# Transposing q in 64x64 tiles instead of 64x128 tiles, in a kernel of linear attention and channel mix on one core

## The chip, the cores and the metric

The kernel runs on one core of a Trainium2 chip. The metric is the time of one execution on the device in microseconds (us); lower is better. Names used below: PE is the matrix engine (TensorE), with its weight loads shown apart as PEld; DVE is VectorE, ACT is ScalarE, POOL is GpSimd, SP is SyncE, which only issues transfers here. SBUF is the on-chip memory that all engines read; PSUM is the small memory that PE writes its results to, in banks; a tile of PSUM must be copied out by ACT or DVE.

A matmul on PE has a weight load (LDWEIGHTS), which puts one operand into the 128x128 array, and the matmul proper (MATMUL), which moves the other operand through it. Operands of 64 rows or 64 columns use only a part of the array, a tile: 64x128 is one half of the rows and all columns, 64x64 a quarter. A transpose is a matmul with the identity as the moving operand.

## What is computed

```python
# q, k, v: (8 batches, 8 heads, 576 tokens, 64)
q_s = softmax(q, over the 64)
k_s = softmax(k, over the 576 tokens)
kv  = k_s^T v                  # 64 x 64 for each batch and head
x   = q_s kv                   # heads joined: (8, 576, 512)
# channel mix; x_prev is x one token back
xk, xr = mu_k * x + (1 - mu_k) * x_prev, mu_r * x + (1 - mu_r) * x_prev
out = sigmoid(xr w_r) * (relu(xk w_k)^2 w_v)   # w_k 512 x 1024, w_v 1024 x 512
```

Inputs and output are float32; inside the kernel the matmuls take bfloat16.

## The kernel before

**Head groups.** The attention is done in sixteen head groups, eight batches (b) of two (g). Each group has four heads: r = 0, 1 lies in the two halves of the 128 partitions of q, k and v (64 partitions each, tokens in the partitions, nine runs of 64 tokens each, j = 0 to 8), and u = 0, 1 is a second index beside it. For a group, ACT takes the exponentials of q and k (L383) and casts v (L389); DVE sums q's (L398), inverts (L402) and scales (L407), which gives the tile qs with 128 columns for each j: the 64 features of u = 0, then the 64 of u = 1.

**On PE, one operation for a group of batches 1 to 7** (`block`, L505) issues, one behind the other:
- X (L591): the product x = q_s kv of the group before, in 64x64 tiles, eight matmuls: four of 64 columns, four of 512. It is there in the blocks from the second group of batch 2 on; batches 0 and 1 get their x in another way (L550).
- T (L417): the transposes of qs, 18 of them, each of 64 rows (r) by 128 columns (both u), into a PSUM half for each r.
- KV (L444): the sums kv, 36 matmuls in 64x64 tiles: for each j, then u, then r, with a column of ones beside v that gives the sum of k's exponentials.

In batch 0, T (L417) and KV (L438 and L441) are operations of their own.

Behind a block, DVE inverts the sums of k (L451) and scales kv (L461), then ACT copies the transposed q out of PSUM to the tile qt (L424). X of this group stands in the next block and waits for that copy. What X writes is copied out by ACT (L597, L600) and mixed with its shift by DVE (L605 to L619).

**The channel mix** is the bulk of PE's work, in matmuls of the full 128x128 array, mostly 512 columns wide: K (L687, xk with w_k), R (L719, xr with w_r) and V (L739, the squares with w_v), four or so to a group of instructions. ACT takes relu (L672) and tanh (L724) out of PSUM, DVE squares (L676) and forms the output (L745), SP stores it (L757).

**Order.** All engines get their instructions in one order, found when the kernel is built: `Plan.order` walks through all operations with their assumed lengths and latencies, takes for each engine what can start first, and among those what is due first; buffers of a pool are handed out on the way. A block's assumed length is a constant in the code (1.1 us, or 0.9 without X), which the change leaves as it is. On the chip each engine goes through its order and waits by semaphores for what an instruction needs. PSUM has four banks "mm" for the channel mix and two pairs of banks "att" for the attention.

Of the kernel before, what the change touches and what calls it, by code (L numbers as in the profile page):

```python
# [81 lines left out]
class Plan:  # L82
# [6 lines left out]
    def add(self, engine, occ, lat, key, emit, deps=(), takes=(), gives=(), size=0.0, rate=1.0,  # L89
            name=""):  # L90
        op = Op(engine, occ, lat, key, emit, [d for d in deps if d is not None], takes, gives,
                size, rate, name)
        self.ops.append(op)
        return op
# [141 lines left out]
def graph(kn):  # L236
# [5 lines left out]
    def in_turn(name):  # L242
        slot = Slot(name)
        slot.rank = ranks.get(name, 0)
        ranks[name] = slot.rank + 1
        return slot
# [59 lines left out]
    identity = add("POOL", 0.6, 0.8, -9.1, lambda: make_identity(kn.nc, kn.ident[:]))  # L306
# [63 lines left out]
    def attention(b, g):  # L370
# [3 lines left out]
        eq, ek, vv, stat, qs, qt, rz = (  # L374
            in_turn(n) if n != "vv" or b else None
            for n in ("eq", "ek", "vv", "stat", "qs", "qt", "rz"))
# [3 lines left out]
        two = (slice(0, 64), slice(64, 128))  # L380
# [30 lines left out]
        def turned(slot, hf):  # L411
            return kn.half(slot, hf).bitcast(BF16)[:, 0:S]

        def transpose_q(slot):
            for j in range(J):
                for r in range(2):
                    kn.nc.tensor.transpose(out=turned(slot, r)[:, 64 * j:64 * j + 64],  # L417
                                           in_=kn.qss[qs.index][two[r], j, :],
                                           identity=kn.ident[two[r], two[r]])

        def copy_qt(slot):
            to = kn.qts[qt.index]
# [72 lines left out]
        if b == 0:  # L495
            qtp, kvp = Slot("any"), Slot("any")
            tr = add("PE", 0.6, 0.7, step, lambda: transpose_q(qtp), before_t, [qtp], [qs],
                     name=f"T{tag}")
            kvm = add("PE", 0.9, 1.0, step, lambda: kv(kvp), before_kv + [tr], [kvp], leave_kv,
                      name=f"KV{tag}")  # L500
        else:
            qtp = kvp = Slot("att")
            turn_x = pending.pop() if pending else None

            def block():  # L505
                if turn_x:
                    turn_x[0](qtp)
                transpose_q(qtp)
                kv(qtp)

            if turn_x:
                tr = kvm = add("PE", 1.1, 1.25, step, block, before_t + before_kv + turn_x[1],
                               [qtp] + turn_x[2], [qs] + leave_kv + turn_x[3], name=f"B{tag}")
                tr.look = BLOCK_LOOK
                turn_x[4](tr, qtp)
            else:
                tr = kvm = add("PE", 0.9, 1.0, step, block,
                               before_t + before_kv + (fused_x if not fused else []), [qtp],
                               [qs] + leave_kv, name=f"TKV{tag}")
# [391 lines left out]
```

## Time and profile before

| | |
|---|---|
| median of 3 runs | 206.15 us (205.49 to 206.4) |
| the profiled execution | 205.87 us |
| its span, first to last instruction | 204.1 us |
| granted clock of PE | 0.995 of full speed |
| busy in the span: PE / DVE / ACT / POOL | 92% / 75% / 72% / 19% |
| T, median of one transpose and of one weight load (L417) | 190 ns, 95 ns |
| KV, median of one matmul and of one weight load (L444) | 192 ns, 107 ns |

The profile is of one execution. Busy time is the time in which an engine has at least one instruction under way; matmuls overlap, so the length of one says little about how many fit into a microsecond, and the distance between starts says more. In a line of the timeline stand the start and the length of a run of like instructions, the engine, the line of the code, the operation, the tile written and the tiles read, the part of the array (rows*columns), the shape of the moving operand and the count. Line numbers are those of the kernel before.

### The profile page before, as it was taken

What the parts mean: (1) busy time and instruction counts of PE and PEld (TensorE: products, weight loads), DVE (VectorE), ACT (ScalarE), POOL (GpSimd) and SP (SyncE); (2) the same over time, 40 slices, a digit from 0 to 9 for tenths busy, and PEclk for the clock granted to TensorE, in tenths of its full rate; (3) what the DMA queues carried; (4) which work ended last, traced back from release to release, by engine and by line L of the source; (5) the groups of instructions that cost most, each with busy time, mean ns of one, the idle gap of its engine ahead of it and who ended that gap; (6) DMA issues with size and microseconds to landing.
All of it is one profiled execution on the core that took longest, in us unless ns stands there. A gap on an engine that the chain in (4) does not pass through costs nothing.

```text
span 204.1 us, 4851 instructions
## 1 busy us (share of the span) xinstructions
PE 187.9 (92%) x1930; PEld 93.9 (46%) x1930; DVE 152.7 (75%) x348; ACT 146.8 (72%) x226; POOL 38.6 (19%) x61
## 2 busy tenths in 40 slices
PE   0659999979999999999999999999999999999990
PEld 0445444534454444444466444444444444444750
DVE  1865478999889989999999995999825459622620
ACT  4463689999999999999999488777624752642520
POOL 4912269433223312532000000000000000000000
PEclk9999999999999999999999999999999999999997
DMA  6999999999999994999742220422044012404303
GB/s 206 277 247 206 256 404 391 399 405 405 392 393 400 410 385 137 368 348 401 224 102 53 48 58 3 100 57 53 0 100 110 0 41 65 103 0 103 90 16 104
DMA packets 16431, 40.10 MB, mean 197 GB/s; under 512 B 2196, under 2 KB 5528, under 8 KB 16408
## 3 DMA queue, kind: packets, MB, share of 16 engines
q0 software_dynamic: 9328, 27.99, 41.6%
q1 hardware_dynamic: 6696, 11.25, 19.7%
q10 hardware_dynamic: 384, 0.56, 0.8%
q8 instruction: 15, 0.25, 0.5%
q14 instruction: 8, 0.07, 0.1%
HBM read 33.56 MB, written 9.44 MB: 211 GB/s over the span
## 4 chain that ended last, share of the span: by engine, by line
PE 78%; DMA 13%; DVE 3%; ACT 2%; POOL 1%; issue 0%; DVEq 0%; ACTq 0%
PE mm_b L739 9%; PE mm_c L739 9%; PE mm_d L739 7%; PE mm_b L687 7%; DMA wr<-in_moe_w_r_dram 7%; PE mm_c L687 7%; PE mm_d L687 7%; PE mm_a L687 7%; PE mm_a L719 6%; DMA raw_g<-in_v_dram 4%; PE mm_a L739 4%; PE mm_d L719 3%; PE mm_c L719 3%; PE mm_b L719 3%; DMA raw_b<-in_q_dram 2%; PE att_b L444 1%
## 5 line engine op out<-in xcount | busy, mean ns | idle before, releaser
L687 PEld LDWEIGHTS <-wk_a 128*128 128x128 bf16 x160 | 15.3, 99 | 17.0 <-issue 1.8
L687 PEld LDWEIGHTS <-wk_b 128*128 128x128 bf16 x160 | 15.5, 98 | 15.3 <-issue 0.2
L719 PEld LDWEIGHTS <-xr 128*128 128x128 bf16 x144 | 13.9, 98 | 16.8 <-ACT xr L563 0.9
L739 PEld LDWEIGHTS <-k_a 128*128 128x128 bf16 x144 | 13.8, 98 | 16.4
L739 PEld LDWEIGHTS <-k_b 128*128 128x128 bf16 x152 | 14.2, 98 | 14.7 <-issue 0.2
L719 PE MATMUL mm_a<-wr,xr 128*128 128x512 bf16 x56 | 14.4, 379 | 0.4 <-DMA raw_g<-in_v_dram 0.4
L724 ACT ACTIVATE th_a<-mm_a 128x512 f32<-128x512 f32 x14 | 8.4, 602 | 7.2 <-PE mm_a L719 7.1
L687 PE MATMUL mm_b<-xk,wk_a 128*128 128x512 bf16 (+1 forms) x44 | 11.2, 371 | 0.0
L687 PE MATMUL mm_c<-xk,wk_a 128*128 128x512 bf16 (+1 forms) x40 | 10.2, 371 | 0.0
L687 PE MATMUL mm_a<-xk,wk_a 128*128 128x512 bf16 (+1 forms) x40 | 9.8, 360 | 0.3 <-DVE xk L560 0.3
L687 PE MATMUL mm_c<-xk,wk_b 128*128 128x512 bf16 (+1 forms) x40 | 9.4, 358 | 0.0
L687 PE MATMUL mm_d<-xk,wk_b 128*128 128x512 bf16 (+1 forms) x40 | 9.4, 358 | 0.0
L687 PE MATMUL mm_a<-xk,wk_b 128*128 128x512 bf16 (+1 forms) x40 | 9.4, 358 | 0.0
L687 PE MATMUL mm_b<-xk,wk_b 128*128 128x512 bf16 (+1 forms) x40 | 9.4, 358 | 0.0
L687 PE MATMUL mm_d<-xk,wk_a 128*128 128x512 bf16 (+1 forms) x36 | 9.2, 368 | 0.0
L315 PE MATMUL mm_a<-mu_rows,pick 2*128 2x512 f32 x2 | 2.0, 1122 | 6.8 <-DMA mu_rows<-in_moe_mu_r_dram 6.8
L719 PE MATMUL mm_d<-wr,xr 128*128 128x512 bf16 x32 | 8.2, 379 | 0.0
L719 PE MATMUL mm_b<-wr,xr 128*128 128x512 bf16 x28 | 7.2, 379 | 0.0
L719 PE MATMUL mm_c<-wr,xr 128*128 128x512 bf16 x28 | 7.2, 379 | 0.0
L676 DVE TENSOR_TENSOR k_a<-rel_a 128x512 bf16<-128x512 bf16 (+1 forms) x13 | 5.1, 391 | 2.8 <-ACT rel_a L672 2.6
L672 ACT ACTIVATE rel_b<-mm_a 128x512 bf16<-128x512 f32 (+1 forms) x7 | 4.0, 571 | 4.1 <-PE mm_a L687 3.9
L676 DVE TENSOR_TENSOR k_a<-rel_c 128x512 bf16<-128x512 bf16 (+1 forms) x13 | 5.1, 392 | 2.4 <-ACT rel_c L672 2.3
(323 smaller groups left out, 487.7 us busy)
## 6 DMA issues: line engine op xcount, KB each, us to landing
out_dram<-ot_a SPq DMA_DIRECT2D x14, 128.0 KB, 2.4
out_dram<-ot_b SPq DMA_DIRECT2D x14, 128.0 KB, 2.4
out_dram<-ot_c SPq DMA_DIRECT2D x14, 128.0 KB, 3.2
out_dram<-ot_d SPq DMA_DIRECT2D x14, 128.0 KB, 2.7
raw_k<-in_v_dram POOLq DMA_DIRECT2D x3, 576.0 KB, 8.5
out_dram<-ot_e SPq DMA_DIRECT2D x13, 128.0 KB, 2.4
raw_j<-in_k_dram POOLq DMA_DIRECT2D x2, 576.0 KB, 10.7
raw_a<-in_q_dram POOLq DMA_DIRECT2D x2, 576.0 KB, 10.1
```

Of the source, the lines that this page charges most:

```text
L315: nc.tensor.matmul(kn.bank(wide_slot), lhsT=kn.pick[:].rearrange("p u c -> p (u c)"), rhs=kn.mu_rows[:].rearrange("p m c -> p (m c)"), sta ...
L444: kn.nc.tensor.matmul(to, lhsT=by, rhs=kn.vvs[vv.index][two[r], j, u, 0:65], **flags)
L672: kn.nc.scalar.activation(out=kn.rels[rel.index][:, 0:n], in_=kn.bank(kf)[:, 0:n], func=ACT.Relu, scale=HALF_ROOT)
L676: kn.nc.vector.tensor_tensor(out=kn.k2s[k2.index][:, fc, 0:n], in0=kn.rels[rel.index][:, 0:n], in1=kn.rels[rel.index][:, 0:n], op=ALU.mult)
L687: kn.nc.tensor.matmul(kn.bank(kf)[:, 0:n], lhsT=kn.wk[fc // 4][:, ct, (fc % 4) * 128:(fc % 4) * 128 + 128], rhs=kn.xs[0][:, ct, c0:c0 + n] ...
L719: kn.nc.tensor.matmul(kn.bank(rps), lhsT=kn.xs[1][:, ct, c:c + 128], rhs=kn.wr[:, ct, :], start=(ct == 0), stop=(ct == CT - 1))
L724: kn.nc.scalar.activation(out=kn.ths[th.index][:], in_=kn.bank(rps), func=ACT.Tanh, scale=0.5)
L739: kn.nc.tensor.matmul(kn.bank(vps)[:, 0:width], lhsT=kn.k2s[k2.index][:, ft, 128 * m:128 * m + 128], rhs=kn.wv[ft // 4][:, ft % 4, part], ...
```

## The change

```diff
         def transpose_q(slot):
             for j in range(J):
-                for r in range(2):
-                    kn.nc.tensor.transpose(out=turned(slot, r)[:, 64 * j:64 * j + 64],
-                                           in_=kn.qss[qs.index][two[r], j, :],
-                                           identity=kn.ident[two[r], two[r]])
+                for u in (two if b else (slice(0, 128),)):
+                    for r in range(2):
+                        kn.nc.tensor.transpose(
+                            out=turned(slot, r)[u, 64 * j:64 * j + 64],
+                            in_=kn.qss[qs.index][two[r], j, u],
+                            identity=kn.ident[two[r], two[r]])
```

`two` is the pair of slices 0 to 63 and 64 to 127. In batches 1 to 7 each transpose of 64x128 becomes two of 64x64, one for each half of the columns; for each j the four follow each other with r as the inner index, as KV's four do. Batch 0 keeps the 64x128 tiles. The result in PSUM is the same, at the same place. PE gets 252 transposes and 252 weight loads more (14 groups, 18 of each); the order of operations and the buffers are those of before on every engine.

## The prediction

> **What bounds the kernel now.** I read the page first, then TensorE's (PE's) waits, then the order of PE's work around one block, and last what ACT does at the same time. The page gives the busy time of each engine and the chain that ended last:
>
> ```profile
> PE 187.9 (92%) x1930; PEld 93.9 (46%) x1930; DVE 152.7 (75%) x348; ACT 146.8 (72%) x226; POOL 38.6 (19%) x61
> PE 78%; DMA 13%; DVE 3%; ACT 2%; POOL 1%; issue 0%; DVEq 0%; ACTq 0%
> ```
>
> The chain is 78% PE; in order of time it is PE alone from 43.2 us to 198.9 us. The view of waits for PE between 50 and 200 us is empty. So a stretch taken out of PE's stream behind 50 us ends the run earlier, unless another engine then makes PE wait. One block, by PE's timeline (start, length, engine, line, operation, tiles, array rows*columns, shape, count):
>
> ```profile
> 59.49 1.03 PE L739 MATMUL mm_d<-wv_b,k_b 128*128 128x512 bf16 x4
> 60.45 0.22 PE L591 MATMUL att_a<-qt_b,w_b 64*64 64x64 bf16 x4
> 60.50 0.39 PE L591 MATMUL att_b<-qt_b,w_b 64*64 64x512 bf16 x4
> 60.82 0.44 PE L417 MATMUL att_a<-ident,qs_a 64*128 64x64 bf16 x18
> 61.19 0.48 PE L444 MATMUL att_a<-vv_b,ek_a 64*64 64x65 bf16 x36
> 61.60 1.04 PE L739 MATMUL mm_b<-wv_a,k_b 128*128 128x512 bf16 x4
> 62.47 1.03 PE L719 MATMUL mm_c<-wr,xr 128*128 128x512 bf16 x4
> ```
>
> The starts matter, since the lengths overlap. L591 is the product x of the former head group (X), L417 the transposes (T), L444 the kv sums (KV). Three things are read from it.
> - **A change of tile costs 0.09 us.** Four 512-column matmuls take 0.865 us (0.216 each), but from the V group at 59.49 to X it is 0.96: 0.095 more. In the single records the last 512-column matmul of X starts at 60.512 and T at 60.824: 0.312, again 0.095 over 0.216. The last pair of T starts at 61.070 and KV at 61.190: 0.120, where a pair follows a pair in 0.029: 0.091. KV to V: 0.12 likewise. Within the 64x64 tile, from X's 64-column to its 512-column matmuls, no such gap stands, nor at 16.32, where batch 0's x product (288 columns, 64x64) is followed by its kv sums (64x64) 0.227 behind, less than the 0.24 in which these products follow each other there (15.37, 15.61, 15.85).
> - **T's step.** Two transposes, one for each row half, start every 0.029 us; 9 steps.
> - **KV's step.** Four 64x64 matmuls with four weight loads start every 0.032 us on average (8 steps in 0.276, the first of them 0.052, while the next weights come in); 36 matmuls in all.
>
> ACT beside it (the same columns):
>
> ```profile
> 58.17 1.20 ACT L389 CAST vv_b<-raw_h 128x1152 bf16<-128x1152 f32 x1
> 59.22 1.16 ACT L424 COPY qt_b<-att_b 128x1152 bf16<-128x1152 bf16 x1
> 60.23 0.65 ACT L724 ACTIVATE th_a<-mm_a 128x512 f32<-128x512 f32 x1
> ```
>
> X at 60.45 reads qt_b, whose copy ended at 60.38: 0.07 us ahead. ACT is then as full as PE. The windows (length, PE, PEld, DVE, ACT, POOL busy) say for how long:
>
> ```profile
> 50.00:61.00 11.00, 11.00 (x188) 5.32 (x182) 9.81 (x21) 11.00 (x16) 3.27 (x5) 1.00 1.03 392
> 61.00:109.00 48.00, 48.00 (x515) 24.26 (x508) 46.67 (x100) 47.38 (x68) 11.58 (x16) 1.00 0.84 299
> 109.00:198.00 89.00, 89.00 (x722) 43.10 (x720) 59.42 (x134) 52.05 (x85) 0.00 (x0) 1.00 0.24 56
> ```
>
> Until 109 us ACT and DVE have next to nothing left; behind it ACT has 37 us free.
>
> **The change, part by part.** Fourteen head groups (batches 1 to 7, two each) get 36 transposes and 36 weight loads in place of 18 and 18. Nothing else is added, moved or made to wait; ACT, DVE, POOL and SP keep their instructions and order.
> 1. *T's own stream.* A step now holds four 64x64 tiles: two row halves by two column halves, in KV's order, with loads of KV's size and moving rows of 64 columns against its 65. Bounds: 0.029 a step (today's pair) and 0.058 (two pairs, one behind the other). I take KV's 0.032, the same instructions but for the transpose: 9 x 0.032 = 0.288 against 9 x 0.029 = 0.261 today and 0.01 more at T's start, so +0.02.
> 2. *X to T.* Both are 64x64: 0.312 becomes about 0.21. -0.10.
> 3. *T to KV.* Both 64x64: the 0.091 goes. KV's long first step (0.052) becomes 0.032, as its weights load behind T: -0.02.
> 4. KV to the next matmul stays at 0.12.
>
> A block with X in front: 0.10 + 0.09 + 0.02 - 0.02 = 0.19 to 0.20; I take 0.20. Of these there are 11 (55.74, 60.45, 70.34, 77.63, 95.29, 101.72, 115.97, 125.85, 129.70, 137.00, 161.56). Without X in front (52.23, and 35.99 and 38.60 in batch 1) the start change of tile stays, and the long first step moves to T: 0.09 + 0.02 - 0.02 - 0.01 = 0.08. The bound for a switch is zero (it stays, rival 1) to the whole 0.19.
>
> The weight loads are the point that speaks against the change:
>
> ```profile
> L417 PEld LDWEIGHTS <-qs_a x108: 92/95/129, 10.3 to 162.2; 64*128 64x128 bf16 x108
> L444 PEld LDWEIGHTS <-ek_c x180: 102/107/111, 36.4 to 138.0; 64*64 64x64 bf16 x180
> ```
>
> A load of half the columns takes 107 ns against 95, and there are twice as many. They overlap, so KV's step, not these lengths, is the price. [...]
>
> *What reaches the end.*
> - Before 50 us PE waits for others (the batch 1 blocks at 35.99 and 38.60 are followed, at 43.16, by a PE wait of 1.2 us for an ACT copy of xk): nothing, whichever way.
> - 50 to 61: 0.08 from 52.23 is kept, since ACT's tanh at 54.08 waits for the R group behind it, and the copy of qt_a that X at 55.74 needs follows on ACT. The 0.20 of the block at 55.74 is lost: X at 60.45 waits for qt_b, and ACT runs from 54.08 to there without a gap. 0.08 left.
> - 61 to 109: five blocks, 1.0 offered. At 108.09 PE needs the bank that ACT's relu at 107.43 (0.40 long) frees, 0.26 ahead. So PE is earlier there by 0.26 more than ACT. ACT is earlier by at least its 0.08, plus what it had itself waited: 0.2 in the waits view (for DVE's w_c) and short waits for matmuls at 72.6, 91.9 and 94.5 that I put at 0.2. PE: 0.34 to 1.1; I take 0.7.
> - 109 to the end: five blocks, 5 x 0.20 = 1.0. The nearest wait is X at 125.85, 0.19 behind a copy that itself follows PE. Kept.
>
> Sum: 0.7 + 1.0 = 1.7 us. The profiled execution took 205.87 (span 204.1 and 1.8 around it), so 204.2; it lay 0.28 below the median of 206.15, on which basis it is 204.4. Bounds of this case: 1.3 (only 0.34 kept by 109) to 2.4 (no wait binds), 203.7 to 204.9.
>
> **The rivals.**
> 1. *The drain belongs to the change between transpose and product, not to the tile.* No row shows a transpose next to a product of the same tile. Then nothing goes and T's step costs +0.03 a block: 12 x 0.03 = +0.4, 206.5. Against it: changes of tile without a transpose (V to X, KV to V) cost the same 0.095, and T's two switches no more.
> 2. *ACT and DVE take more of it.* Blocks to 109 give 0 and one or two later ones are lost at X (slacks of 0.19 at 125.85, 0.55 at 129.70): gain 0.4 to 1.0, 205.4. For it: the full ACT above. Against: 37 us of room behind 109.
> 3. *The instructions do not come fast enough* (the slower side). From X to the end of KV PE starts 160 instructions where there were 124 in 1.03 us (8.3 ns each); the forecast wants them in 0.83, 5.2 ns each. Batch 0's kv sums hold 6.6 ns over 144 (four every 0.053 us, at half today's pace), KV 4 ns over 72 only, which a buffer may have held. If the supply were 8.3 ns, a block takes 1.33: +0.3, 12 times, +3.6: 209.8. It decides from 6.4 ns on, where 160 take today's time.
>
> ```profile
> 13.98 0.26 PE L438 MATMUL att_b<-vb_a,ek_a 64*64 64x64 bf16 x4
> 14.03 0.21 PE L441 MATMUL att_a<-one,ek_a 64*64 64x1 bf16 x4
> 14.09 0.26 PE L438 MATMUL att_b<-vb_a,ek_a 64*64 64x64 bf16 x4
> ```
>
> 4. *The added transposes stand in line.* If the column halves do not run side by side, a step is 0.058: T 0.52, a block 0.03 slower than now even without the drains, 206.5; with each of the 18 alone at 0.029, 0.3 slower, 209.8. Against it: KV's four tiles start 0.0035 apart. [...]
>
> **How the numbers follow.** Half a percent, 1.0 us, is about what a measurement of this kernel can tell from no change. Forecast 0.64 (all of it faster), rival 1 0.13 and rival 2 0.09 (same), rival 3 0.08 (slower), rival 4 0.06 (half same, half slower). Faster 0.64, same 0.25, slower 0.11. The range takes in the forecast's bounds, rivals 1 and 2 and the mild half of 4: 203.6 to 206.6.
>
> **What would show it.** Right: the transposes as 64*64 x36, T 0.22 behind X's 512 columns (now 0.32), KV 0.29 behind T (now 0.37), the next group 0.39 behind KV (now 0.41), and new PE waits for ACT near 60 and 108 us. Wrong: 0.31 and 0.12 still standing around T (rival 1), T's step above 0.055 (rivals 3 and 4), or a block 0.20 shorter with the end less than 1 us earlier (rival 2).

## The result, and the profile after

The changed kernel takes 207.56 us in the median of 20 runs (206.53 to 211.04), the kernel before 206.01 (204.92 to 206.84). The ratio is 1.0071, 95% interval 1.0048 to 1.0094: slower by 1.5 us, where 1.7 us less was forecast. Four runs of over 210 us, with a granted clock of 0.982 to 0.983 against 0.984 to 1.000 in the others, are left out of the ratio. The profiled execution took 207.04 us (span 205.3).

The page's busy times and chain:

```profile
PE 183.7 (90%) x2158; PEld 94.0 (46%) x2182; DVE 152.2 (74%) x348; ACT 146.7 (71%) x226; POOL 38.5 (19%) x61
PE 49%; issue 1%; ACT 0%; DVE 0%
```

The kernel has 2182 matmuls, one for each weight load, and 2158 of them are recorded; the 24 that are missing leave short gaps in the view (0.16 us) that are no waits. The chain is PE alone again, but is lost half way back, at a place without a releaser.

The blocks did what was forecast of them, the end did not. PE's timeline of one block, in the columns of the view before:

```profile
61.93 1.03 PE L741 MATMUL mm_d<-wv_b,k_b 128*128 128x512 bf16 x4
62.88 0.22 PE L593 MATMUL att_a<-qt_b,w_b 64*64 64x64 bf16 x4
62.94 0.39 PE L593 MATMUL att_b<-qt_b,w_b 64*64 64x512 bf16 x4
63.16 0.48 PE L418 MATMUL att_a<-ident,qs_a 64*64 64x64 bf16 x36
63.45 0.49 PE L446 MATMUL att_a<-vv_b,ek_a 64*64 64x65 bf16 x36
```

T starts 0.22 behind X's 512 columns where it was 0.32, KV 0.29 behind T where it was 0.37. But one block earlier the same view shows this:

```profile
56.81 0.37 PE L418 MATMUL att_b<-ident,qs_c 64*64 64x64 bf16 x20
57.00 0.45 PE L446 MATMUL att_b<-vv_a,ek_c 64*64 64x65 bf16 x32
59.17 0.22 PE L446 MATMUL att_b<-vv_a,ek_c 64*64 64x65 bf16 x4 [1.72 <-issue]
```

Of KV's 36 matmuls 32 are issued, then PE stands for 1.9 us between two weight loads (57.23 to 59.17), in the middle of an operation that waits for nothing. In the square brackets stand the idle time and its releaser; "issue" means that the profile knows none. PE's waits, largest first:

```profile
PE mm_a L315 <- DMA mu_rows<-in_moe_mu_r_dram: 7.5, 1, 7.5
PE att_b L446 <- issue: 1.7, 1, 1.7
PE att_a L443 <- ACT qt_a L426: 1.0, 1, 1.0
PE att_a L552 <- DVE wp_a L540: 1.0, 1, 1.0
```

The first and third were there before. The second is the standstill just shown. The fourth is new as well: a product of batch 1 (L552) that starts at 42.36 where it started at 41.21. PE's row for it, and DVE's for what it reads:

```profile
42.36 0.44 PE L552 MATMUL att_a<-qt_c,wp_b 64*64 64x288 bf16 x8 [0.96 <-DVE wp_a L540]
```

```profile
38.46 0.90 DVE L540 TENSOR_TENSOR wp_b<-kvn_a,mu_wide 128x128 bf16<-128x128 f32 x4
39.66 0.20 DVE L534 COPY qt_c<-qt_c 128x126 bf16<-128x126 bf16 x1 [0.31 <-ACT qt_c L426]
```

It reads wp_b and qt_c, not wp_a; they were done at 39.36 and 39.86, 2.5 us ahead. The releaser named is only what ended last on DVE by then.

**What stands at both places** shows in the number of the instruction. Counting PE's weight loads and matmuls from the start of the program (two instructions for each weight load, since each has its matmul), PE stops behind the 956th and behind the 1468th: 512 apart. The trace's DMA records hold instruction transfers as packets of 16,384 bytes on queue 8 (the page's "q8 instruction": 15 packets before, 17 after, for 504 instructions more, some 250 to a packet). The author's estimate is 256 to a packet, from the 512 between the two stops if two packets lie between them; 956 is then 444 + 2 x 256 and 1468 is 444 + 4 x 256. So if 444 instructions are there at the start, the third packet brings the 957th instruction and the fifth the 1469th. The 444 is chosen to fit these two places. The count leaves out PE's other instructions (waits on semaphores, for one), so that it gets rougher with every packet. From those records (us):

```
                        packet 3 landed   next instr.   packet 5 landed   next instr.
before                  40.79             44.44         57.83             61.38
changed                 41.13             42.36 stood   57.83             59.17 stood
```

Before, PE came to these instructions 3.6 us behind their packets. The changed kernel comes there earlier and goes on 1.2 to 1.3 us after the packet has landed. By this reading PE had run out of instructions; the experiments test it.

### The profile page after: what moved, and what is told of

It is laid out like the page before. It is cut to its first block, busy times and chain, and to the rows that moved or that the text cites. A ratio compares the mean times of both kernels' runs of the same rounds, so it can differ in the third digit from the quotient of the medians.

```text
span 205.3 us, 5331 instructions
## 1 busy us (share of the span) xinstructions
PE 183.7 (90%) x2158; PEld 94.0 (46%) x2182; DVE 152.2 (74%) x348; ACT 146.7 (71%) x226; POOL 38.5 (19%) x61
## 4 chain that ended last, share of the span: by engine, by line
PE 49%; issue 1%; ACT 0%; DVE 0%
PE mm_c L741 7%; PE mm_b L741 6%; PE mm_b L689 5%; PE mm_c L689 4%; PE mm_d L741 4%; PE mm_a L689 4%; PE mm_d L689 4%; PE mm_a L721 3%; PE mm_a L741 3%; PE mm_d L721 3%; PE mm_b L721 2%; PE mm_c L721 1%; PE att_a L593 1%; PE att_b L593 1%; PE att_b L446 1%
## 5 line engine op out<-in xcount | busy, mean ns | idle before, releaser
L689 PE MATMUL mm_d<-xk,wk_a 128*128 128x512 bf16 (+1 forms) x34 | 8.7, 367 | 0.3 <-issue 0.3
L674 ACT ACTIVATE rel_c<-mm_a 128x512 bf16<-128x512 f32 (+1 forms) x7 | 4.0, 567 | 4.3 <-PE mm_a L689 4.3
L678 DVE TENSOR_TENSOR k_a<-rel_b 128x512 bf16<-128x512 bf16 (+1 forms) x14 | 5.7, 405 | 1.7 <-ACT rel_b L674 1.6
```

Source lines behind the costliest of these rows:

```text
L674: kn.nc.scalar.activation(out=kn.rels[rel.index][:, 0:n], in_=kn.bank(kf)[:, 0:n], func=ACT.Relu, scale=HALF_ROOT)
L678: kn.nc.vector.tensor_tensor(out=kn.k2s[k2.index][:, fc, 0:n], in0=kn.rels[rel.index][:, 0:n], in1=kn.rels[rel.index][:, 0:n], op=ALU.mult)
L689: kn.nc.tensor.matmul(kn.bank(kf)[:, 0:n], lhsT=kn.wk[fc // 4][:, ct, (fc % 4) * 128:(fc % 4) * 128 + 128], rhs=kn.xs[0][:, ct, c0:c0 + n] ...
```

## The experiments

The theory after this (supply): the added instructions bring PE to the end of its stock before the next packet is usable, because the packets come slowly behind the loads of q, k and v. The rival (tile): 64x64 transposes disturb PE where they stand. Each edit is to the changed kernel, unless said otherwise.

**e1_from2 and e8_from2_again: 64x64 from batch 2 on.**

```diff
-                for u in (two if b else (slice(0, 128),)):
+                for u in (two if b >= 2 else (slice(0, 128),)):
```

> 64x64 transposes from batch 2 on; batch 1 keeps 64x128, as batch 0 does, so 36 loads and 36 matmuls fewer than the changed kernel. Supply theory: PE ran out of instructions twice in the changed kernel's profile (1.0 us at its 956th, 1.9 us at its 1468th load-or-matmul instruction), because batch 1's and 2's extra instructions brought those points forward to before the next 16 KB of instructions had come. With 72 fewer, both points come later than the fetch: no stall, every block about 0.2 us shorter, 203.8 to 205.0 where before is 206.0. Tile theory (64x64 transposes disturb PE wherever they stand in a dense stretch): eleven of the blocks are as they were, so the time stays near 207.5, at most 0.3 less.

> 64x64 transposes from batch 2 on, again, on the chip of the last kernel for the comparison: 1.0 to 1.4 us faster than the kernel before, no stall.

Measured: 204.31 us against 205.35 (ratio 0.9943, 0.9923 to 0.9963), and again 204.18 against 205.66 (0.9934, 0.9911 to 0.9957). PE's waits have no line of "issue" and none for wp_a; in e1's profile the packets land at 40.40 and 56.74, and PE comes to the two places at 43.90 and 60.11, 3.5 and 3.4 us behind them. The second place now lies in the T of this block, which runs through:

```profile
59.86 0.41 PE L593 MATMUL att_b<-qt_b,w_b 64*64 64x512 bf16 x4
60.08 0.49 PE L418 MATMUL att_a<-ident,qs_a 64*64 64x64 bf16 x36
60.39 0.49 PE L446 MATMUL att_a<-vv_b,ek_a 64*64 64x65 bf16 x36
```

All eleven blocks with X are as in the changed kernel, so the tile theory is wrong. What was taken back is 36 weight loads and 36 transposes, in two groups that PE had to wait behind anyway.

**e2_only12: 64x64 in batches 1 and 2 only.**

```diff
-                for u in (two if b else (slice(0, 128),)):
+                for u in (two if b in (1, 2) else (slice(0, 128),)):
```

> 64x64 transposes in batches 1 and 2 only. Supply theory: the same two stalls as in the changed kernel and next to none of the gain (0.1 to 0.3 us): 207.5 to 209.5. Tile theory: four of fourteen blocks changed, so about four fourteenths of the 1.5 us: 206.3 to 206.6, and no stall that stands out at the 956th and 1468th instruction.

Measured: ratio 1.0160 (1.0110 to 1.0211), by the three of six runs that took 207.2 to 209.7 us; the other three took 211.7, 212.1 and 253.4, and the profile is of the first of these. PE stood behind the 956th and the 1468th instruction again (1.85 and 2.10 us from one weight load to the next).

**e3_pad12: the old tiles, each transpose of batches 1 and 2 issued twice.**

```diff
-                for u in (two if b else (slice(0, 128),)):
+                for u in (slice(0, 128),) * (2 if b in (1, 2) else 1):
```

> The tiles of the kernel before (64x128 everywhere), but in batches 1 and 2 each transpose is issued twice, which writes the same values again: as many instructions as with 64x64 tiles there, no change of tile saved, and T 0.26 us longer in each of four blocks, of which two lie where PE is not the bound. Supply theory: the two stalls of the changed kernel appear without any 64x64 transpose, 207.5 to 210. Tile theory: no stall, 206.1 to 206.6.

Measured: 208.47 us, ratio 1.0145 (1.0111 to 1.0178). PE's timeline of it, the same columns; the array part of T is 64*128, and KV breaks off at the same matmul:

```profile
58.10 0.70 PE L418 MATMUL att_b<-ident,qs_c 64*128 64x64 bf16 x36
58.73 0.45 PE L446 MATMUL att_b<-vv_a,ek_c 64*64 64x65 bf16 x32
60.40 0.22 PE L446 MATMUL att_b<-vv_a,ek_c 64*64 64x65 bf16 x4 [1.23 <-issue]
```

No 64x64 transpose is in this kernel, and PE stands behind the 956th (1.34 us from load to load) and the 1468th instruction (1.45) as before. So it is the number of instructions that brings PE to a stop, not the tile. Part of the 3.0 us is the added work itself: T takes 0.51 us instead of 0.25 in four blocks.

**e4_after_again: the changed kernel, unaltered.**

> The changed kernel again, for a second profile. Supply theory: stalls at the same two instructions (956 and 1468), of other lengths, since the fetch queues behind loads: each 0.5 to 3 us; 206.5 to 208.5 in all. Tile theory: stalls elsewhere or none.

Measured: 208.19 us, ratio 1.0118 (1.0079 to 1.0158) on this chip. Behind the 956th and 1468th instruction PE stood 1.89 and 2.35 us. What this profile shows beside it is told at the end.

**e5_light_after, e6_light_before, e10_light_after2: the loads cut.** Batches 2 to 7 load 8 of 576 columns for each partition, but for their first load, and compute on old data; e6 is the same in the kernel before.

```diff
-                         ap=[[J * D, 128], [4 * S * D, u.stop - u.start], [1, J * D]])
-            return kn.queues[engine].dma_start(out=kn.raws[slot.index][:, u, :], in_=ap)
+                         ap=[[J * D, 128], [4 * S * D, u.stop - u.start], [1, 8 if (b, g, i) > (2, 0, 0) else J * D]])
+            return kn.queues[engine].dma_start(
+                out=kn.raws[slot.index][:, u, 0:8 if (b, g, i) > (2, 0, 0) else J * D], in_=ap)
```

> The changed kernel (64x64 in batches 1 to 7) with the loads of batches 2 to 7 cut to 8 of 576 columns for each partition, but for the first one, so that the DMA engines are near idle from about 35 us on; the other engines work on old data, as before in kind and order. Supply theory: PE's 16 KB fetches start at once where they took 3.5 us to start behind the loads, so the stalls at the 956th and 1468th instruction go, though the instructions are those of the changed kernel, and it is 1.3 to 2.3 us faster than the kernel before under the same light loads. If the count of instructions alone stalled PE (its own rate of taking them in), the two stalls would stay.

> The kernel before with the same cut loads, for comparison. PE is the bound from 53 us on with or without the loads, so 204 to 206, no stall in it under either theory.

> The changed kernel with cut loads again, for a profile: no stall of PE at the 956th and 1468th instruction, the fetches there starting within 1.5 us of PE's entry into its last 256 instructions; near 204.2.

Measured: e5 204.17 us (0.9930 of the kernel before, 0.9905 to 0.9954), e6 205.46 (0.9997, 0.9973 to 1.0021). The profiled execution of e5 took 1,069.6 us, five times the others, and is not read. e10 gave 204.95 us in one execution, no "issue" among PE's waits, and this block:

```profile
56.24 0.22 PE L594 MATMUL att_b<-qt_a,w_a 64*64 64x64 bf16 x4
56.27 0.41 PE L594 MATMUL att_a<-qt_a,w_a 64*64 64x512 bf16 x4
56.49 0.50 PE L419 MATMUL att_b<-ident,qs_c 64*64 64x64 bf16 x36
56.80 0.49 PE L447 MATMUL att_b<-vv_a,ek_c 64*64 64x65 bf16 x36
57.23 1.04 PE L742 MATMUL mm_c<-wv_b,k_b 128*128 128x512 bf16 x4
```

It is the block that broke off, with all 36 of KV in one run. The windows of the two kernels around the two places say what differs (length, PE, PEld, DVE, ACT, POOL, then the clock, the busy share of the DMA engines and GB/s), first the changed kernel, then e10:

```profile
36.00:41.00 5.00, 4.79 (x159) 2.82 (x160) 4.55 (x17) 4.71 (x8) 2.46 (x4) 1.00 1.04 397
...
52.00:58.00 6.00, 5.29 (x164) 2.90 (x163) 5.42 (x10) 6.00 (x9) 1.45 (x2) 1.00 1.04 390
```

```profile
36.00:43.00 7.00, 6.58 (x179) 3.43 (x178) 6.56 (x23) 6.70 (x9) 3.17 (x5) 1.00 0.41 89
...
50.00:58.00 8.00, 8.00 (x194) 4.13 (x193) 7.32 (x15) 7.97 (x12) 1.44 (x2) 1.00 0.09 8
```

By the count above, the third and fifth packet start 3.6 and 3.5 us after PE has come to its last 256 instructions in the changed kernel, with full DMA engines; in e10 it is 1.3 and 0.8 us, and PE comes to the two places 2.7 and 2.1 us behind the packets. The instructions of both are the same, so PE's own rate of taking them in is not what stops it: with the loads out of the way the packets come in time.

**e7_from3: 64x64 from batch 3 on.**

```diff
-                for u in (two if b else (slice(0, 128),)):
+                for u in (two if b >= 3 else (slice(0, 128),)):
```

> 64x64 transposes from batch 3 on. The two blocks of batch 2 were reckoned at 0.08 us together (one without X, one whose gain ACT takes at the next X): 0 to 0.2 us slower than with batch 2 included (204.3). No stall. If batch 2's blocks gave their full 0.28, it would be 0.3 slower.

Measured: 204.88 us, ratio 0.9951 (0.9924 to 0.9977), beside 204.18 for e8 in the same comparison. The intervals overlap; it lies in the direction of batch 2 giving something, and cannot tell 0.1 from 0.3.

**e9_not2: 64x64 in batch 1 and from batch 3 on.**

```diff
-                for u in (two if b else (slice(0, 128),)):
+                for u in (two if b not in (0, 2) else (slice(0, 128),)):
```

> 64x64 transposes in batch 1 and from batch 3 on; batch 2 keeps 64x128. By the count of instructions (supply theory) batch 1's 72 still bring the 956th instruction to 40.8 us, before the third fetch is usable at about 42.3: PE stands 1 to 2 us there, and gets part of it back, since the product behind it waits for ACT at 43.2 in any case. The 1468th instruction then lies in the block at about 61, behind the fifth fetch: no stall there. 204.5 to 206.5: slower than without batch 1's (204.2), faster than the changed kernel. If the stalls went with the blocks of batch 2 and not with the count, there would be none, and 204.2.

Measured: 205.95 us, ratio 1.0006 (0.9980 to 1.0032). PE stood behind the 956th instruction (1.66 us from load to load, packet 3 at 41.57, PE at 42.81). It came to the 1468th at 61.97, 3.7 us behind packet 5, and did not stand. e1 has batch 2 in 64x64 tiles and no stop, e9 has it in the old tiles and one: what decides is not the block, but whether PE has used up its instructions before the next packet can be used. And batch 1's 72 extra instructions alone eat about what the later blocks gain.

## Why the prediction was wrong, point by point

**The drain belongs to the tile: right.** X to T fell from 0.312 to 0.209 between starts, T to KV from 0.120 to 0.025. Rival 1 (the drain goes with the transpose) and rival 4 (the added transposes in line) are out: T's 36 take 0.271 from first to last start, where 18 took 0.246.

**A block's gain: right in kind, a fifth too large.** From X's last matmul to KV's last it was 0.312 + 0.246 + 0.120 + 0.287 = 0.965, and in most blocks is 0.209 + 0.271 + 0.025 + 0.295 = 0.800: 0.165 less, against 0.20. T's own 0.025 more is as forecast. KV did not get shorter by its long first step (0.295 against 0.287). In the KV at 57.0 of the changed kernel a pair of load and matmul starts every 8.3 ns, 4.2 ns an instruction, against 4.0 in KV's step before (0.032 for eight, which is the mean of the seven steps behind the first; with the first it is 0.0345). So KV as a whole keeps its old length, though its first step is no longer a long one.

**What ACT takes: right.** In e1, without the stops, the places can be read off PE's starts against those of the kernel before: the gain of the block at 55.74 (0.17) is lost at the next X, as worked out (X at 59.83 stands 0.05 behind ACT's copy of qt_b), and 0.24 again near 107, where 0.4 had been allowed for: the matmuls at 106.87 start 0.68 behind the group before them, not 0.44, and ACT's relu that frees their bank ends at 106.81. The view of waits has no line for either, because the matmul before is recorded as still running. From 52 us to the last matmul e1 gains 1.3 us in the profiles; both measured ratios stand for 1.2 and 1.4 us. Of the 1.7 that was forecast the rest went with the 0.20 that is 0.165, and with two delays of 0.1 inside KV, in the blocks that stood at 115.97 and 129.70 before: KV takes 0.40 there from first to last start instead of 0.29. These delays stay unexplained: they stand near the same matmul of the block in every kernel with 64x64 transposes there, with cut loads (e10) as well.

**The step that failed** is "Nothing else is added, moved or made to wait", and with it "Before 50 us ... nothing, whichever way". The 36 weight loads and 36 transposes added in batch 1, and the same in batch 2, bring forward the moment at which PE needs its next packet of instructions. The changed kernel against from-batch-2: ratios of 1.0071 and 1.0118 against 0.9943 and 0.9934, some 2.6 to 3.8 us for the stops and what follows them (3.6 in the one comparison that has both, e4 and e1). The two blocks of batch 1, reckoned at nothing, cost some 1.1 us by e9 against e7 (1.0006 against 0.9951, with intervals that do not meet), about as much as the later blocks bring.

**Rival 3 named the cause and mis-sized it.** It spoke of a steady rate, priced by the pace within a block (8.3 ns an instruction, a loss of 0.3 in each of 12 blocks, deciding from 6.4 ns on). No such rate is in the trace: PE takes 4.2 ns where the instructions are there, but for the two delays of 0.1. What runs short is the stock, at two places out of seventeen packets, and it had its sign in the trace of before, unread: in the DMA records of queue 8, where by the same count packets 1, 3 and 5 land 2.0, 3.6 and 3.6 us ahead of their use, and all others 8 to 27 us. Its chance of 0.08 left the result, 207.56, 1 us outside the range.

## What to carry to other kernels

Where PE's instructions get smaller and more, look at when its instruction packets land and when their first instruction is due, as one would with any load: here a dense stretch needed the next packet while the DMA engines were full of data (390 to 397 GB/s in the changed kernel), and PE stood 1.3 to 2.4 us from one weight load to the next (the nine stops of five profiles). An "issue" wait in the middle of one operation, at the same count of instructions in several kernels, was the sign of it here; the other stop was put down to an engine whose work the matmul did not read. Spend added instructions only where the shorter stretch reaches the end: leaving out batch 1 turned 0.7% slower into 0.6% faster, and that version (from batch 2 on, 204.2 to 204.3 us) beats both kernels.

## What the runs showed of the hardware

- **Change of tile.** 0.091 to 0.095 us of PE's time between instructions of different tiles, whether transposes or products (the block at 60.45 of the kernel before); between 64x64 products and 64x64 transposes nothing (in the changed kernel starts 0.209 apart for 512 columns, against 0.216 within a tile).
- **Instruction packets.** They are of 16,384 bytes each; that one holds some 256 of PE's weight loads and matmuls is the estimate above, beside 252 by the two packets more for 504 instructions more. PE goes on 1.2 to 1.6 us after the packet has landed (nine stops in five profiles). By the count above, the packets of these nine stops start 3.4 to 3.8 us after PE's entry into its last 256 instructions, with full DMA engines; with cut loads packets 3 and 5 start 1.3 and 0.8 us after it (e10). At which moment a packet is asked for stays open: packet 5 of the kernel before starts 0.9 us after that entry although the DMA engines are as full (390 GB/s from 55.7 to 57.9), and some later packets start up to 4.4 us ahead of it, where the count is rough.
- **The clock after a stop.** In e4's profile the granted clock is at half behind each of the two stops (columns as in the windows above; the clock is the third number from the end):

```profile
40.76:44.18 3.42, 1.63 (x32) 0.85 (x32) 2.50 (x7) 3.02 (x4) 1.09 (x3) 1.00 1.04 409
44.18:47.59 3.41, 3.41 (x16) 1.06 (x9) 3.26 (x4) 2.10 (x3) 1.39 (x2) 0.50 1.03 400
57.83:61.24 3.41, 1.27 (x81) 0.98 (x80) 1.59 (x2) 2.52 (x4) 0.72 (x1) 1.00 1.03 386
61.24:64.66 3.42, 3.42 (x13) 1.18 (x10) 1.84 (x5) 2.34 (x3) 0.72 (x1) 0.50 0.90 340
```

 It is the same in e2's profile (half from 44.15 and from 61.22, for 3.41 us each), and in no other of the eleven profiles that were read, but for the end of the program. In the 3.41 us ahead of each fall, by the first and third line above, PE was idle for 1.79 and 2.14 us. The length of the stop alone does not decide: e2's stop of 1.85 us was followed by a fall, the changed kernel's of 1.94 was not (granted clock 1.00 from 20.6 to 204.8 us). What does decide was not shown. The spread of the changed kernel's runs fits stops with and without a fall: the granted clock was 0.995 to 1.000 in the runs of up to 207.4 us, 0.984 to 0.992 in those of 207.7 to 208.9, and 0.982 to 0.983 in those of over 210.
